# A fused attention and maxout kernel on one core: the order of batch 0's scores, weight transposes and block products, and the PSUM banks of its first up blocks

## The chip, the cores and the metric

The kernel runs on one NeuronCore of a Trainium2 chip. The metric is the device time in microseconds (us) of one execution, as a median over runs. A core has a matrix engine (TensorE, "PE" in the profile, with its weight loads as "PEld"), a vector engine (VectorE, "DVE"), an activation engine (ScalarE, "ACT"), GpSimd ("POOL", which here issues the loads), and SyncE ("SP", which issues stores and small DMAs). Each engine works through its own instructions in the order in which the program gives them; semaphores hold one back until another engine's result is there. TensorE writes only to PSUM, of which the kernel uses eight banks.

## The reference, cut to what matters

Eight batches of Linformer attention (keys and values are projected from 1024 positions to 64), followed by a maxout layer without biases:

```python
k_proj = np.einsum('ks,bhsd->bhkd', E, k)          # 8 batches, 8 heads, 1024 positions, 64 wide
v_proj = np.einsum('ks,bhsd->bhkd', F, v)
scores = scale * np.matmul(q, k_proj.transpose(0, 1, 3, 2))
attn   = softmax(scores)                            # over the 64 projected positions
x      = np.matmul(attn, v_proj)                    # then rows of 512: (8192, 512)
out    = np.maximum(x @ w1, x @ w2) @ w_out         # w1, w2: 512 x 1024; w_out: 1024 x 512
```

The kernel uses max(a, b) = relu(a - b) + b: with wd = w1 - w2 and M = w2 @ w_out it computes relu(x @ wd) @ w_out + x @ M. Most of the large products are done by a seven-product scheme for 2x2 blocks (Winograd's form of Strassen's), with sums of blocks made on VectorE.

## The kernel before, in words

The order of the work is written out by hand; no scheduler moves anything. Batches 1 to 7 run in a steady pipeline. All that the change touches is batch 0's start, whose steps stand in one list (L992 to L1041), followed by a list of small functions called `slots` (L1069 to L1082), which runs before the steady pipeline.

**The start.** Batch 0's heads are worked on in two groups g (four heads each) and two halves j of the positions. For each (g, j) the steps are: `step_sc` (scores: eight matmuls at L343 into two PSUM banks, then Exp on ACT, L383), `step_dn` (sums of the exponentials, eight matmuls at L355, then Ln on ACT, L391), `step_inv` (Exp of minus that, L430, and a small DMA), and `step_at` (the values: sixteen matmuls at L355, then two multiplications on DVE, L446, which write `xt`, the rows x of the reference turned on their side). `step_kv(..., "v")` projects v, 16 matmuls for every two heads (L197); the projection of heads 4 to 7 is copied to `vp` by ACT (L209), those of heads 0 to 3 by DVE. The loads of v come in four DMAs of two heads each. `warm(n)` are n matmuls without a use.

**The up blocks.** `up_slots(t, j)` (L519) gives eight blocks fb for each half j, here called u0[fb] and u1[fb]. One is four matmuls of 128x512 (L528, r = 0 to 3, of which r = 0, 1 need the head group g = 0 and r = 2, 3 need g = 1) into one PSUM bank, and then a relu out of the bank: on ACT at L537, for fb = 3 on DVE at L539. The first two blocks of each half are done in two pieces: the pieces r = 0, 1 of u0[0], u1[0], u0[1], u1[1] in this order (L1038), later the pieces r = 2, 3 of u0[0], u0[1], then of u1[0], u1[1] (L1070 to L1072).

**w2 on its side.** `step_w2t(f0)` (L556) transposes eight 128x128 pieces of w2 on TensorE (L560) into one bank, and ACT copies 128x1024 of them to `w2t_sb` (L568). There are four such steps; that of f0 = 768 leaves its copy for later (`box["w2t"]`).

**The seven-product parts.** S1, S2, S6, S5, S7, S3, S4 are the products of the second half of the up blocks of half 1 (L766); M1 to M4 are those of M (L644). DVE makes their block sums (L607, L719), wd (L544, L552) and the additions.

**PSUM banks.** Four banks are named mm0 to mm3, and two pairs form the rotating buffer "att". `mm_bank()` without a number takes the first of the list `turn` and puts it at the end; with a number it takes that bank. A new tile in a bank waits until the last reader of the bank's previous tile is done. By the time of L1037 `turn` is [0, 1, 2, 3], so that `first_banks` gives u0[0] and u0[1] the banks 0 and 1, u1[0] and u1[1] the banks 2 and 3. Every later up block takes bank fb % 2 (L524):

```python
t["up", j, fb] = mm_bank(n=first_banks[j][fb] if r1 < NDC else fb % 2)
```

S1 takes bank 2, S2 takes bank 3, M2 takes bank 0 and M5 bank 1.

Of the kernel before, what the change touches and what calls it, by code (L numbers as in the profile page):

```python
# [10 lines left out]
FP16 = mybir.dt.float16  # L11
# [8 lines left out]
def kernel(  # L20
# [12 lines left out]
    nc = tc.nc  # L33
# [29 lines left out]
    turn = [0, 1, 2, 3]  # L63

    def mm_bank(dtype=FP32, n=None):
        if n is None:
            n = turn.pop(0)
            turn.append(n)
        return ps.tile([128, 512 if dtype == FP32 else 1024], dtype, tag=f"mm{n}", name="mm_ps")

    def att_banks(dtype=FP32):
        return ps.tile(
            [128, 2, 512 if dtype == FP32 else 1024], dtype, tag="att", bufs=2, name="att_ps"
        )
# [4 lines left out]
    def big(n, dtype=FP16):  # L79
        return const.tile([128, 16384 // mybir.dt.size(dtype) // 2], dtype, tag=f"big{n}", name=f"big{n}")  # L80
# [45 lines left out]
    w2_sb = big(2).rearrange("p (r f) -> p r f", r=NDC)  # L126
    wo_sb = const.tile([128, NFB, DM], FP16, tag="wo", name="wo_sb")
    for g in range(2):
        for w_sb, w in ((w2_sb, moe_w2), (w1_sb, moe_w1)):
            nc.gpsimd.dma_start(  # L130
                out=w_sb.rearrange("p (g z) f -> p g z f", z=2)[:, g, :, 0:256],
                in_=w.rearrange("(g p z) f -> p g z f", p=128, z=2)[:, g, :, 0:256],
            )
    for w_sb, w, f0, f1 in (
# [3 lines left out]
        for z in range(2):  # L138
            nc.gpsimd.dma_start(
                out=w_sb.rearrange("p (g z) f -> p g z f", z=2)[:, :, z, f0:f1],  # L140
                in_=w.rearrange("(g p z) f -> p g z f", p=128, z=2)[:, :, z, f0:f1],
# [16 lines left out]
    ident16 = const.tile([128, 128], FP16)  # L158
# [26 lines left out]
    def step_kv(t, h0=0, h1=H, which="kv", att=False, dma=False, copy=nc.vector.tensor_copy, between=None):  # L185
        kv_ps = att_banks()[:, 0, :] if att else mm_bank(n=0 if dma else None)
        n = (h1 - h0) * D
        both = which == "v"
        nh = 2 if both else h1 - h0
        for h in range(0, h1 - h0, nh):  # L190
            if h and between is not None:
                between()
            for c in range(NC):
                for w in which:
                    i = "kv".index(w)
                    for r in range(2) if both else (i,):
                        nc.tensor.matmul(  # L197
                            out=kv_ps[r * KP : (r + 1) * KP, h * D : (h + nh) * D],
                            lhsT=eft[i][:, c, :],
                            rhs=t[w][:, h0 + h : h0 + h + nh, c, :],  # L200
                            start=(c == 0), stop=(c == NC - 1),
                        )
        zd = lambda ap: ap.rearrange("p (h d z) -> p h z d", d=D // 2, z=2)
        if "k" in which:
            eng = nc.vector.tensor_copy if which == "k" or dma else nc.scalar.copy
            kp = t["kp"][:, h0:h1]
            eng(out=kp[:, :, 0, :], in_=kv_ps[0:KP, 0:n].rearrange("p (h d) -> p h d", d=D))
        if both:
            copy(out=t["vp"][:, h0:h1], in_=zd(kv_ps[:, 0:n]))  # L209
        elif "v" in which:  # L210
            def finish_v():
                nc.vector.tensor_copy(out=t["vp"][KP:128, h0:h1], in_=zd(kv_ps[KP:128, 0:n]))
                if dma:
                    nc.vector.tensor_copy(out=kp[:, :, 1, :], in_=kp[:, :, 0, :])
                    step_kpt_dma(t)
                else:
                    step_vp(t, h0, h1)

            if att:
                return finish_v  # L220
            finish_v()


    def step_vp(t, h0=0, h1=H):
        fl = lambda ap: ap[:, h0:h1].rearrange("p h z d -> p (h z d)")
        nc.vector.tensor_copy(out=fl(t["vp"][0:KP]), in_=fl(t["vp"][KP:128]))
# [71 lines left out]
    def step_kpt_dma(t):  # L298
        nc.sync.dma_start_transpose(
            out=t["kpt"], in_=t["kp"].rearrange("p h r d -> p (h r d)")  # L300
        )
# [60 lines left out]
    def sums_into(t, g, j, dn_ps):  # L362
        tiles_into(lambda o: dn_ps[:, o, :], t["ex", g, j], lambda rows, hh: ones16[rows, 0:Z])
# [15 lines left out]
    def step_sc(t, g, j):  # L379
        sc_ps = att_banks()  # L380
        t["ps", g, j] = sc_ps
        score(t, g, j, [sc_ps[:, e, :] for e in range(2)])
        nc.scalar.activation(out=t["ex", g, j], in_=sc_ps, func=ACTF.Exp, scale=scale)  # L383

    def step_dn(t, g, j):
        dn_ps = t.pop(("ps", g, j))[:, :, 0:W]
        sums_into(t, g, j, dn_ps)
        ld = (ppool.tile([128, 2, W], FP32, tag="pd", bufs=4, name="ld_sb") if t is tiles[0]
              else soft.tile([128, 2, W], FP32, tag="soft", name="ld_sb"))
        t["ld", g, j] = ld  # L390
        nc.scalar.activation(out=t["ld", g, j], in_=dn_ps, func=ACTF.Ln)  # L391
# [36 lines left out]
    def step_inv(t, g, j):  # L428
        ld = t["ld", g, j]
        nc.scalar.activation(out=ld, in_=ld, func=ACTF.Exp, scale=-1.0)  # L430
        check(ld)
# [84 lines left out]
    w2t_sb = big(3).rearrange("p (f m) -> p f m", f=NFB)  # L516
# [32 lines left out]
    def step_wd_rows(f0):  # L549
        for z in range(2):  # L550
# [2 lines left out]
                out=rows(wd_sb), in0=rows(w1_sb), in1=rows(w2_sb), op=ALU.subtract  # L553
            )

    def step_w2t(f0, att=False, hold=False):  # L556
        ps_t = att_banks(FP16)[:, 0, :] if att else mm_bank(FP16)
        for f in range(2):
            for r in range(NDC):
                nc.tensor.transpose(  # L560
                    out=ps_t[:, (f * NDC + r) * 128 : (f * NDC + r + 1) * 128],
                    in_=w2_sb[:, r, f0 + f * 128 : f0 + (f + 1) * 128],
                    identity=ident16,
                )
        fb = f0 // 128

        def copy():
            nc.scalar.copy(  # L568
                out=w2t_sb[:, fb : fb + 2, :].rearrange("q f m -> q (f m)"), in_=ps_t
            )  # L570

        if hold:
            box["w2t"] = copy
        else:
            copy()
# [9 lines left out]
    CH = DM // 2  # L585
    units = [(b, o) for b in range(B) for o in range(2)]
    last = len(units) - 1
    U = {(b, o): {"n": n, "b": b, "o": o, "t": tiles[b]} for n, (b, o) in enumerate(units)}
# [4 lines left out]
    box = {}  # L593
# [15 lines left out]
    def step_t(part, which=range(4)):  # L609
        n0, n1, src = ((0, NG, wo_sb), (NG, NG + NX, m_sb))[part]  # L610
        hs = n1 - n0
        sub4(
            [T_sb[:, i, n0:n1, :] for i in range(4)],
            lambda h, c: src[:, h * hs : (h + 1) * hs, c * CH : (c + 1) * CH], which,
        )
# [6 lines left out]
    def sums_m(i):  # L622
        m_sums[i] = ppool.tile([128, NG, CH], FP16, tag="pd", bufs=4, name="p_sb")
        sum_s(lambda j, h: m_blk(j, h), lambda n: m_sums[n], i)
# [100 lines left out]
    def sums_x(u, which):  # L725
        step_s(u, x_blk, lambda i: s_x(i, u), which)

    def sums_g(u, which):
        step_s(u, g_blk, s_g, which)
# [262 lines left out]
    t = tiles[0]  # L992
# [26 lines left out]
    warm(2)  # L1019
    step_sc(t, 1, 0)  # L1020
    step_kv(t, 0, 2, "v")
    step_kv(t, 2, 4, "v")
    step_dn(t, 1, 0)
    step_sc(t, 1, 1)
    step_at(t, 0, 0)
    step_at(t, 0, 1)
    step_inv(t, 1, 0)
    step_kv(t, 4, 8, "v", True, copy=nc.scalar.copy, between=lambda: step_dn(t, 1, 1))
    step_inv(t, 1, 1)
    att_banks()  # L1030
    for f0 in (0, 128):
        step_wd(f0, 0, 2, 128)
    step_at(t, 1, 0, True)
    u0, u1 = [*up_slots(t, 0)], [*up_slots(t, 1)]
    step_wd(0, 2, 4)
    step_at(t, 1, 1, True)
    first_banks = turn[0:2], turn[2:4]  # L1037
    for i in range(2):  # L1038
        for u in u0, u1:
            u[i](r1=2)  # L1040
    step_w2t(0, True)  # L1041


    load_all(tiles[1], 1, "k", k)
# [1 line left out]
    wd = [lambda f0=f0: step_wd_rows(f0) for f0 in range(0, DF, 256)]  # L1046
    f = lambda s, *a: lambda: s(tiles[0], *a)

    def loads(b, *names):
# [17 lines left out]
    S1, S2, S6, S5, S7, S3, S4 = up_steps(U[0, 1], (1,))  # L1067
    M1, M2, M6, M5, M7, M3, M4, M_add = m_steps()
# [2 lines left out]
        lambda: step_w2t(256, True),  # L1071
        lambda: u1[0](r0=2), lambda: u1[1](r0=2), wd[1], lambda: sums_x(U[0, 1], range(4)),  # L1072
        u0[2], u0[3], S1, S2, lambda: step_w2t(512, True), lambda: step_w2t(768, True, True), wd[2],
        u0[4], u0[5], lambda: box.pop("w2t")(), wd[3],
        lambda: [step_tw(i, 1) for i in range(2)] and None, lambda: U[0, 1]["c0"](),
        lambda: [step_tw(i, 1) for i in range(2, 4)] and None,
        u1[4], S6, u1[5], S5, u0[6], S7, u0[7],
        lambda: [sums_m(i) for i in range(4)] and None, S3, S4,
        lambda: step_t(0, (0, 1)), M1, lambda: step_t(0, (2, 3)), M2, lambda: sums_x(U[0, 0], (0, 1)),
        M6, lambda: sums_g(U[0, 0], (0, 1)), M_add, M5, lambda: sums_g(U[0, 0], (2, 3)), M7, M3, M4,  # L1080
        lambda: (open_box(3), new_attn(tiles[1]), turn.__setitem__(slice(None), [2, 3])) and None,
    ]  # L1082
# [32 lines left out]
    t = tiles[1]  # L1115
    for n, x in enumerate((
# [4 lines left out]
        for name in x.split():  # L1121
# [6 lines left out]
            else:  # L1128
                g, j = int(name[2]), int(name[3])
# [14 lines left out]
    t = tiles[2]  # L1144
# [8 lines left out]
    for b in range(3, B):  # L1153
        t = tiles[b]
# [25 lines left out]
    for n, (b, o) in enumerate(units):  # L1180
# [14 lines left out]
        if n:  # L1195
            end = ("U", n - 1, 1, 6) if n > 1 else ("P", 0, 6, 1)
            m = 0 if n == last else 2
# [17 lines left out]
    for key, slot in slots:  # L1215
        r = slot()
        pending = [g for g in [r, *(f() for f in pending)] if g is not None]
        for s in steps.pop(key, ()):
            r = s()
# [5 lines left out]
    for reg in regs:  # L1225
# [4 lines left out]
        out=mm_bank()[0:1, 0:1], lhsT=ones16[:, 0:1], rhs=ones16[:, 0:1], start=True, stop=True  # L1230
# [166 lines left out]
```

## Time and profile before

| what | value |
|---|---|
| median of 3 runs | 319.62 us (319.59 to 319.87) |
| the profiled execution's own time | 319.29 us |
| its span (first to last instruction) | 317.5 us |
| granted TensorE clock, mean | 0.999 |
| PE busy | 311.7 us (98%) |
| PEld busy | 254.9 us (80%) |
| DVE busy | 244.9 us (77%) |
| ACT busy | 206.9 us (65%) |

The profile is of one execution. A row of its timeline gives the start in us from the span's start, the time to the end of the last of the instructions that it merges, the engine, the source line, the operation, output<-input, the shape and the count; in brackets stands how long the engine was idle before it, and what released it. Matmuls are pipelined, so that a row's time overlaps the next row's start; what one matmul costs is read from the starts. A busy engine is not an engine at its peak.

### The profile page before, as it was taken

Reading aid. Unit: us, or ns where it says so; the run is one execution under the profiler, and the core shown is the slowest. Engines: PE = TensorE matmul, PEld = TensorE weight load, DVE = VectorE, ACT = ScalarE, POOL = GpSimd, SP = SyncE. Lnnn points to the kernel's source line nnn. Section 1 sums busy time; section 2 is a strip of 40 time slices with the busy share of each in tenths; the row PEclk is TensorE's granted clock in tenths of the full one; section 3 lists DMA queues with packets and bytes.
Section 4 is the critical chain, followed back from the end, with each engine's and each line's share of the span. In section 5 each row is a group of like instructions: output and inputs, shape, how many; then the busy total and the mean of one; then the engine's idle time right before and its main releaser. Section 6 shows DMA issues by size and latency. Waiting matters only on the chain.

```text
span 317.5 us, 9309 instructions
## 1 busy us (share of the span) xinstructions
PE 311.7 (98%) x3902; PEld 254.9 (80%) x3902; DVE 244.9 (77%) x474; ACT 206.9 (65%) x375; POOL 39.7 (13%) x63
## 2 busy tenths in 40 slices
PE   7989999999999999999999999999999999999996
PEld 3656688788887888788887888788887888888885
DVE  3368997977969696996969696996969696969883
ACT  2477843767776777477776777476776777765541
POOL 8269002011000400003000300003000000000000
PEclk9999999999999999999999999999999999999999
DMA  8999999999978799997999699987998431313134
GB/s 190 206 201 199 207 206 202 208 166 165 185 144 193 135 195 245 235 190 118 226 242 243 124 199 246 218 164 124 224 222 204 90 101 36 103 34 102 35 102 136
DMA packets 76685, 53.72 MB, mean 169 GB/s; under 512 B 29664, under 2 KB 76128, under 8 KB 76640
## 3 DMA queue, kind: packets, MB, share of 16 engines
q0 software_dynamic: 30688, 28.05, 56.2%
q1 hardware_dynamic: 45664, 24.85, 31.5%
q8 instruction: 31, 0.51, 0.7%
q10 hardware_dynamic: 288, 0.20, 0.2%
q14 instruction: 14, 0.11, 0.1%
HBM read 57.15 MB, written 16.78 MB: 233 GB/s over the span
## 4 chain that ended last, share of the span: by engine, by line
PE 92%; DMA 5%; POOL 1%; ACT 1%; issue 0%; DVE 0%; POOLq 0%
PE mm_ps L874 47%; PE mm_ps L766 28%; DMA v_sb<-in_v_dram 4%; PE att_ps L355 3%; PE mm_ps L528 3%; PE mm_ps L197 3%; PE mm_ps L343 2%; PE att_ps L239 1%; PE att_ps L644 1%; PE mm_ps L644 1%; DMA out_dram<-o_sb 1%; PE mm_ps L313 1%; PE att_ps L560 1%; POOL k_sb L108 0%; POOL q_sb L108 0%; ACT ld_sb L391 0%
## 5 line engine op out<-in xcount | busy, mean ns | idle before, releaser
L736 ACT COPY p_sb<-mm_ps 128x512 f32<-128x512 f32 x180 | 102.4, 592 | 47.3 <-PE mm_ps L766 27.2
L874 PEld LDWEIGHTS <-big 128*128 128x128 f16 x768 | 73.5, 98 | 11.8 <-issue 3.6
L874 PE MATMUL mm_ps<-T_sb,big 128*128 128x256 f16 x576 | 76.9, 273 | 0.0
L781 DVE TENSOR_TENSOR gt_sb<-mm_ps,p_sb 128x512 f16<-128x512 f32 x58 | 39.9, 688 | 42.8 <-PE mm_ps L766 41.4
L766 PE MATMUL mm_ps<-big,big 128*128 128x256 f16 x348 | 52.2, 273 | 0.0
L766 PEld LDWEIGHTS <-big 128*128 128x128 f16 x464 | 45.4, 98 | 5.9 <-DVE big L607 0.2
L874 PE MATMUL mm_ps<-wo_sb,gt_sb 128*128 128x256 f16 x256 | 42.6, 273 | 0.0
L874 PEld LDWEIGHTS <-gt_sb 128*128 128x128 f16 x376 | 35.7, 98 | 6.7 <-issue 2.7
L472 ACT ACTIVATE ex_sb<-mm_ps 128x512 f16<-128x512 f32 x50 | 27.2, 596 | 18.0 <-PE mm_ps L343 12.3
L766 PEld LDWEIGHTS <-wd_sb 128*128 128x128 f16 x348 | 34.1, 98 | 4.4
L766 PE MATMUL mm_ps<-xt_sb,wd_sb 128*128 128x256 f16 x232 | 33.8, 273 | 0.0
L502 DVE TENSOR_TENSOR xt_sb<-att_ps,ld_sb 128x1024 f16<-128x1024 f32 x26 | 31.7, 1218 | 0.2
L874 PE MATMUL mm_ps<-m_sb,xt_sb 128*128 128x256 f16 x128 | 24.5, 273 | 0.0
L905 DVE TENSOR_TENSOR o_sb<-mm_ps,p_sb 128x512 f32<-128x512 f32 x32 | 21.8, 683 | 2.8 <-ACT p_sb L934 2.0
L784 DVE TENSOR_SCALAR gt_sb<-gt_sb 128x512 f16<-128x512 f16 (+1 forms) x62 | 21.8, 351 | 2.1
L305 POOL COPY junk<-qt_sb 1x1 f16<-1x1 f16 x6 | 1.4, 238 | 174.1 <-DMA qt_sb<-q_sb 174.1
L719 DVE TENSOR_TENSOR big<-gt_sb 128x1024 f16<-128x1024 f16 x32 | 21.8, 682 | 0.0
L874 PE MATMUL mm_ps<-wo_sb,big 128*128 128x256 f16 x128 | 21.5, 273 | 0.0
L843 ACT ACTIVATE gt_sb<-mm_ps 128x512 f16<-128x512 f32 x29 | 17.4, 600 | 5.9 <-PE mm_ps L766 5.9
L874 PE MATMUL mm_ps<-T_sb,gt_sb 128*128 128x256 f16 x120 | 20.3, 273 | 0.0
L781 DVE TENSOR_TENSOR gt_sb<-p_sb 128x512 f16<-128x512 f32 x29 | 19.8, 682 | 0.6 <-ACT p_sb L736 0.6
L874 PEld LDWEIGHTS <-xt_sb 128*128 128x128 f16 x188 | 18.3, 98 | 2.3 <-issue 0.2
(123 smaller groups left out, 432.9 us busy)
## 6 DMA issues: line engine op xcount, KB each, us to landing
out_dram<-o_sb SPq DMA_DIRECT2D x62, 256.0 KB
k_sb<-in_k_dram POOLq DMA_DIRECT2D x7, 1024.0 KB, 10.2
v_sb<-in_v_dram POOLq DMA_DIRECT2D x7, 1024.0 KB, 17.0
q_sb<-in_q_dram POOLq DMA_DIRECT2D x5, 1024.0 KB, 23.5
q_sb<-in_q_dram POOLq DMA_DIRECT2D x6, 512.0 KB, 16.1
big<-in_moe_w_dram POOLq DMA_DIRECT2D x12, 128.0 KB, 6.5
v_sb<-in_v_dram POOLq DMA_DIRECT2D x4, 256.0 KB, 13.4
wo_sb<-in_moe_w_out_dram POOLq DMA_DIRECT2D x1, 1024.0 KB, 10.3
```

Source lines behind the costliest of these rows:

```text
L197: nc.tensor.matmul(out=kv_ps[r * KP : (r + 1) * KP, h * D : (h + nh) * D], lhsT=eft[i][:, c, :], rhs=t[w][:, h0 + h : h0 + h + nh, c, :], ...
L355: nc.tensor.matmul(out=dst(r ^ (hh % 2))[hh * Z : (hh + 1) * Z, :], lhsT=weights(rows, hh), rhs=ex[rows, hh % 2, hh // 2 * W : (hh // 2 + ...
L472: nc.scalar.activation(out=t["ex", g, j][:, e, :], in_=banks[e], func=ACTF.Exp, scale=scale)
L502: nc.vector.tensor_tensor(out=x_out(t, g, j).rearrange("q z o n -> q o z n"), in0=at_ps.rearrange("q o (z n) -> q o z n", z=2), in1=ld[:, ...
L719: nc.vector.tensor_tensor(out=S(i), in0=S(0) if x is None else x, in1=y(), op=op)
L736: copy(out=x, in_=bank)
L766: nc.tensor.matmul(out=bank[:, m * W : (m + 1) * W], lhsT=w_[:, n_, (2 * d + m) * 128 : (2 * d + m + 1) * 128], rhs=a[:, n_, :], start=(n ...
L781: nc.vector.tensor_tensor(out=c_blk(j, c), in0=two(x), in1=two(y), op=ALU.add)
L784: nc.vector.tensor_scalar_max(ap, ap, 0.0)
L843: nc.scalar.activation(out=out, in_=in_, func=ACTF.Relu)
L874: nc.tensor.matmul(out=bank[i][:, 0:CH] if two_banks else bank[:, i * CH : (i + 1) * CH], lhsT=a(c)[:, i * 128 : (i + 1) * 128], rhs=w_(c) ...
L905: nc.vector.tensor_tensor(out=o_sb, in0=two(x), in1=two(y), op=ALU.add)
```

## The change

Lines are of the changed kernel where marked with +. It does four things to batch 0.

1. The scores of (1, 1) are moved ahead of the projection of v's heads 2 and 3; their sums (`step_dn(t, 1, 1)`) are moved from the middle of the projection of heads 4 to 7 to ahead of it. On ACT the Exp of (1, 1) thereby comes ahead of the Ln of (1, 0).
2. The eight transposes of `step_w2t(0)` are split in two halves by the rows of w2. The first four (`step_w2t_half(0, ...)`) are issued right after the last projection of v, into bank mm0; ACT's copy of them comes after the Exp of `step_inv(t, 1, 1)`. The other four stand where all eight stood.
3. `first_banks` becomes banks 1 and 2 for u0[0], u0[1], and 3 and 0 for u1[0], u1[1].
4. In `slots`, u1[4] and u1[5] come ahead of S6, the others of that stretch follow in another order, S3 comes after M1 and S4 after M2; ACT's held copy of w2's transposes comes after u1[4] instead of after u0[5].

The numbers of matmuls, transposes, DMAs and DVE instructions stay as they are. One 128x1024 copy on ACT becomes two of 128x512. The instructions on POOL and SP keep their order.

```diff
+    def step_w2t_half(g, ps_t):
+        for f in range(2):
+            for z in range(2):
+                r = 2 * g + z
+                nc.tensor.transpose(
+                    out=ps_t[:, (f * 2 + z) * 128 : (f * 2 + z + 1) * 128],
+                    in_=w2_sb[:, r, f * 128 : (f + 1) * 128], identity=ident16,
+                )
+        return lambda: nc.scalar.copy(
+            out=w2t_sb[:, 0:2, g * CH : (g + 1) * CH],
+            in_=ps_t[:, 0 : 2 * CH].rearrange("q (f m) -> q f m", f=2),
+        )
+
...
     step_sc(t, 1, 0)
     step_kv(t, 0, 2, "v")
+    step_sc(t, 1, 1)
     step_kv(t, 2, 4, "v")
     step_dn(t, 1, 0)
-    step_sc(t, 1, 1)
     step_at(t, 0, 0)
     step_at(t, 0, 1)
     step_inv(t, 1, 0)
-    step_kv(t, 4, 8, "v", True, copy=nc.scalar.copy, between=lambda: step_dn(t, 1, 1))
+    step_dn(t, 1, 1)
+    step_kv(t, 4, 8, "v", True, copy=nc.scalar.copy)
+    w2t_copy = step_w2t_half(0, mm_bank(FP16, turn[0]))
     step_inv(t, 1, 1)
+    w2t_copy()
     att_banks()
...
-    first_banks = turn[0:2], turn[2:4]
+    first_banks = turn[1:3], (turn[3], turn[0])
     for i in range(2):
         for u in u0, u1:
             u[i](r1=2)
-    step_w2t(0, True)
+    step_w2t_half(1, att_banks(FP16)[:, 0, :])()
...
-        u0[4], u0[5], lambda: box.pop("w2t")(), wd[3],
+        u0[4], u0[5], wd[3],
...
-        u1[4], S6, u1[5], S5, u0[6], S7, u0[7],
-        lambda: [sums_m(i) for i in range(4)] and None, S3, S4,
-        lambda: step_t(0, (0, 1)), M1, lambda: step_t(0, (2, 3)), M2, lambda: sums_x(U[0, 0], (0, 1)),
+        u1[4], lambda: box.pop("w2t")(), u1[5], S6, u0[6], S5, u0[7], S7,
+        lambda: [sums_m(i) for i in range(4)] and None,
+        lambda: step_t(0, (0, 1)), M1, S3, lambda: step_t(0, (2, 3)), M2, S4, lambda: sums_x(U[0, 0], (0, 1)),
```

## The prediction

> **What bounds the kernel now.** I read the page first, then the busy times of a long stretch, then TensorE's waits behind the start.
>
> ```profile
> span 317.5 us, 9309 instructions
> PE 92%; DMA 5%; POOL 1%; ACT 1%; issue 0%; DVE 0%; POOLq 0%
> ```
>
> The chain of work that ended last is TensorE for 92% of the span. The 5% DMA lie at the start (v) and at the end (the last store). The busy times from 22.60 to 308.60 us (columns: stretch, its length, busy us of PE, PEld, DVE, ACT, POOL, granted clock, DMA) and all waits of PE behind 22.7 us show how tight that is:
>
> ```profile
> 22.60:308.60 286.00, 285.99 (x3578) 238.16 (x3579) 231.45 (x426) 194.45 (x356) 27.20 (x41) 1.00 0.88 168
> ```
>
> ```profile
> PE mm_ps L1229 <- DMA out_dram<-o_sb: 1.2, 1, 1.2
> PE att_ps L355 <- ACT vp_sb L209: 0.5, 1, 0.5
> ```
>
> PE is busy for 285.99 of 286.00 us at full clock, and waits only for v's cast (before 22.61) and for the last store. So whatever moves PE after 22.61 us moves the end by as much: a microsecond of new wait is a microsecond of time, since no old wait is left to take it up. What can be gained lies in three things only: the start at 22.61, the 0.47 us wait ahead of it, and the work behind it.
>
> The start on PE, in order of time:
>
> ```profile
> 18.77 0.64 PE L197 MATMUL mm_ps<-v_sb,eft 128*64 128x128 f16 x16 [0.45 <-DMA v_sb<-in_v_dram]
> 19.34 0.30 PE L355 MATMUL att_ps<-ex_sb,ones 64*32 64x256 f16 x8
> 19.57 0.41 PE L343 MATMUL att_ps<-qt_sb,kpt_sb 64*64 64x256 f16 x8
> 19.91 0.63 PE L355 MATMUL mm_ps<-ex_sb,vp_sb 64*32 64x256 f16 x32
> 20.47 0.64 PE L197 MATMUL att_ps<-v_sb,eft 128*64 128x128 f16 x16
> 21.27 0.30 PE L355 MATMUL att_ps<-ex_sb,ones 64*32 64x256 f16 x8 [0.16 <-ACT ex_sb L383]
> 21.50 0.64 PE L197 MATMUL att_ps<-v_sb,eft 128*64 128x128 f16 x16
> 22.61 0.63 PE L355 MATMUL att_ps<-ex_sb,vp_sb 64*32 64x256 f16 x32 [0.47 <-ACT vp_sb L209]
> 23.21 1.90 PE L528 MATMUL mm_ps<-xt_sb,wd_sb 128*128 128x512 f16 x8
> 24.95 0.61 PE L560 MATMUL att_ps<-ident,big 128*128 128x128 f16 x8
> 25.39 1.03 PE L528 MATMUL mm_ps<-xt_sb,wd_sb 128*128 128x512 f16 x4
> 26.26 0.61 PE L560 MATMUL att_ps<-ident,big 128*128 128x128 f16 x8
> 26.70 2.75 PE L528 MATMUL mm_ps<-xt_sb,wd_sb 128*128 128x512 f16 x12
> 29.29 1.04 PE L766 MATMUL mm_ps<-xt_sb,wd_sb 128*128 128x256 f16 x8
> ```
>
> Starts give the prices: eight transposes cost 25.39 - 24.95 = 0.44 us, one 128x512 matmul (29.29 - 26.70) / 12 = 0.216. The last row holds the second pieces of u1[0] and u1[1] (four matmuls), then u0[2] and u0[3]; u0[2] starts at 26.70 + 4 x 0.216 = 27.56.
>
> **Part 1, scores and sums moved.** The scores of (1, 1) fill the 0.45 us wait for v ahead of 18.77 (their row takes 0.34 from start to start), and their Exp on ACT no longer holds up the sums at 21.27. What is late next are the loads of v, VectorE's copy of v, and VectorE itself:
>
> ```profile
> 19.01 0.71 POOL L139 DMA_DIRECT2D big<-in_moe_w_dram  x1 [1.41 <-DMA v_sb<-in_v_dram]
> 21.54 0.71 POOL L139 DMA_DIRECT2D big<-in_moe_w_dram  x1 [0.62 <-DMA v_sb<-in_v_dram]
> ```
>
> ```profile
> 19.45 0.29 DVE L209 CAST vp_sb<-mm_ps 128x128 f16<-128x128 f32 x1 [0.79 <-PE mm_ps L197]
> 20.47 2.48 DVE L446 TENSOR_TENSOR xt_sb<-mm_ps,ld_sb 128x512 f16<-128x512 f32 x4 [0.73 <-PE mm_ps L355]
> 22.87 0.48 DVE L544 TENSOR_TENSOR wd_sb<-big,big 128x256 f16<-128x256 f16 x2
> 24.80 1.28 DVE L446 TENSOR_TENSOR xt_sb<-att_ps,ld_sb 128x512 f16<-128x512 f32 x2
> ```
>
> POOL went on at 19.01 for the same load that let PE go at 18.77, so it is 0.24 late; the last pair of v, for which POOL waited until 21.54, then landed at about 21.30. Its projection ran at 21.50, so this end gains 0.20 at most. The values of (0, 0) need v's copy, done at 19.45 + 0.29 = 19.74; with 0.06 for the hand-over (ACT's cast of 22.18 + 0.37 = 22.55 let PE go at 22.61; its row stands below) they start at 19.80 instead of 19.91. VectorE's multiplications follow 0.56 behind (19.91 to 20.47) and then run without a gap to 26.08 (24.80 + 1.28), so all of them come 0.11 earlier. u0[0] needs the first wd of 22.87 and thus also starts 0.11 earlier, at 23.10. I take -0.11; the bounds are 0 (v's copy comes no sooner) and -0.20 (v's landing).
>
> **Part 2, four transposes moved.** They go from PE's full stretch into the wait ahead of the values of (1, 0): -0.22. They fit: four take 0.22 us, the wait has 0.47. u0[0]'s second piece then starts at 25.39 - 0.11 - 0.22 = 25.06. The eight transposes of w2t(256) would start at 25.93, but their bank is read by the multiplications that end at 26.08 - 0.11 = 25.97; with a hand-over of 0.05 they start at 26.02, 0.24 earlier than now. Without any other change u0[2] would then start at 27.32.
>
> **Part 3, the banks.** This is the term that decides. u1[1] now sits in bank 0, and u0[2] takes bank fb % 2 = 0 as before. Until now bank 0 held u0[0], whose relu is the first in ACT's order; now it holds u1[1], whose relu is the fourth, behind the 128x1024 copy of w2t(256). In the built programs u0[2]'s first matmul waits for ACT's 17th counted instruction before, u0[0]'s relu, and for the 22nd after, u1[1]'s; ACT's order is half copy, half copy, relu of u0[0] and u0[1], copy of w2t(256), relu of u1[0] and u1[1]. ACT now:
>
> ```profile
> 22.18 0.37 ACT L209 CAST vp_sb<-att_ps 128x256 f16<-128x256 f32 x1
> 22.45 0.63 ACT L430 ACTIVATE ld_sb<-ld_sb 128x512 f32<-128x512 f32 x1
> 25.59 1.01 ACT L568 COPY big<-att_ps 128x1024 f16<-128x1024 f16 x1 [2.51 <-PE att_ps L560]
> 26.50 1.09 ACT L537 ACTIVATE gt_sb<-mm_ps 128x512 f16<-128x512 f32 x2
> 27.47 1.03 ACT L568 COPY big<-att_ps 128x1024 f16<-128x1024 f16 x1
> 28.36 1.62 ACT L537 ACTIVATE gt_sb<-mm_ps 128x512 f16<-128x512 f32 x3
> ```
>
> The rows give: PE's end to ACT's start 0.20 (the transposes' last slot ends at 25.39, the copy starts at 25.59); a 128x1024 copy takes 0.89 to the next start (27.47 to 28.36), two relus 0.97 (26.50 to 27.47), one relu 0.60 to its end (1.09 for two that start 0.49 apart). The second half's transposes end at 25.06, so:
>
> - second half copy starts at 25.26. No row has a 128x512 copy of f16. Between the 128x256 cast (0.27 from 22.18 to the next start at 22.45) and the 128x1024 copy (0.89) I take the 0.49 of the 128x512 relus, which have its size: next start 25.75. With 0.27 the relu would still wait for PE, until 25.06 + 0.43 + 0.20 = 25.69; with 0.89 it starts at 26.15. So -0.06 or +0.40.
> - relus of u0[0], u0[1]: 25.75 + 0.97 = 26.72. The copy's transposes end at 26.02 + 0.44 = 26.46, and with 0.20 that is 26.66: no wait.
> - copy of w2t(256): 26.72 + 0.89 = 27.61.
> - relu of u1[0]: 27.61; of u1[1]: 28.10, to its end 28.70; hand-over 0.06: u0[2] starts at 28.76.
>
> Against 27.56 that is **+1.20 us**; PE stands still for 28.76 - 27.32 = 1.44. Behind u0[2] in PE's queue is all the rest, and no wait is left that takes it up.
>
> If bank 0's copy of the first half were late it would hold u1[1]'s first piece; it starts behind the Exp of (1, 1), at about 22.8, and has until 23.10 + 6 x 0.216 = 24.40. No cost.
>
> **Part 4, the new order.** It removes no wait, because PE has none there now. It adds round trips: u1[5] now directly follows u1[4] and waits for bank 1, which u0[5]'s relu frees.
>
> ```profile
> 31.06 2.75 PE L528 MATMUL mm_ps<-xt_sb,wd_sb 128*128 128x512 f16 x12
> 32.99 0.60 ACT L537 ACTIVATE gt_sb<-mm_ps 128x512 f16<-128x512 f32 x1 [0.27 <-PE mm_ps L528]
> ```
>
> u0[5] ends at 31.06 + 8 x 0.216 = 32.79; its relu runs to 33.59 and with 0.06 the bank is free 0.86 behind the block's end, which is just the time of the block between (4 x 0.216). u1[4] does the same now without a wait, so I put 0, with +0.05 as the other end. ACT's held copy comes two relus later, and the sums of w2 on VectorE behind it:
>
> ```profile
> 34.98 0.69 DVE L719 TENSOR_TENSOR p_sb<-big 128x1024 f16<-128x1024 f16 x1
> 38.23 0.69 DVE L607 TENSOR_TENSOR T_sb<-wo_sb,T_sb 128x1024 f16<-128x1024 f16 x1
> 40.17 1.04 PE L644 MATMUL att_ps<-T_sb,p_sb 128*128 128x256 f16 x8
> ```
>
> With PE 1.20 later, u1[4] ends at 33.65 + 1.20 = 34.85 (33.65 is where the row of 31.06 ends by starts), its relu starts at 35.05, the copy at 35.54 and ends near 36.5; VectorE's sums start 1.5 later than 34.98, so 0.3 later against PE. M6 at 40.17 has 1.25 us to spare behind T's row (38.92): cover enough. Without it, 0.3.
>
> **Sum.** -0.11 - 0.22 + 0.09 (bank of w2t(256)) + 1.44 = +1.20. The profiled execution took 319.29 us for a span of 317.5 (1.79 around it): 318.7 + 1.79 = 320.5. It lies 0.33 under the median of the runs; the median becomes 319.62 + 1.20 = 320.8.
>
> **The rivals.**
>
> 1. *The bank is free in time (not slower).* One mechanism, at L524: if u1[1]'s relu ends by 27.26, u0[2] doesn't wait, and -0.11 - 0.22 + 0.09 = -0.24 remains: 319.4 us. It decides from 1.44 us on: so much shorter must ACT's row from the half copy to u1[1]'s relu be. For it speaks that ACT is idle before 25.59 for 2.51 us; against it that the five instructions ahead can't start before their matmuls of 25.06 to 26.46, and that the rows leave 0.06 us of air in 3.5. This is also the case in which the change does what its words say and nothing else. 8 in 100.
> 2. *The clock falls in the new wait.* PE's opening shows what a slow clock costs:
>
> ```profile
> 1.47 3.60 PE L153 MATMUL mm_ps<-ones 128*128 128x512 f16 x8 [1.47 <-DVE ones L146]
> 5.00 1.14 PE L169 MATMUL mm_ps<-ident,big 64*128 64x64 f32 x8
> ```
>
> Eight matmuls take 3.53 us there by starts, 0.44 each, against 0.216 later, so a repetition costs 3.53 - 8 x 0.216 = 1.8: 322.6 us. Against it: the wait of 0.47 us just ahead of 22.61 was followed by a clock of 1.00 in the row of the long stretch. No row shows a wait of 1.4. 4 in 100.
>
> The Trainium skill, "TensorE: Matmul & The Clock Gate", section "What's actually happening", says that the array's clock is halved after an idle window of about 3.4 us. By that rule a wait of 1.44 us is too short, and this rival doesn't come; no run here shows yet whether that holds for such a wait.
>
> 3. *ACT's queue is shorter or longer than I lay it out,* by a copy of another price or a relu that starts otherwise: a part of the stall, some +0.3 (319.9), 4 in 100; or with the round trips of part 4 and the slow half copy +1.7 (321.3), inside the range.
>
> **How the numbers follow.** Forecast 320.8, 81 in 100 with its own spread; rival 1 8, rival 2 4, a part of the stall 4, something longer 3. The range takes -0.09 (front gain of 0.20) and +0.40 + 0.05 + 0.11 from the unknown costs, widened at the low end for the hand-overs read from single rows: 320.3 to 321.4. About 0.2% (0.64 us) is what a measurement of this kernel can tell from no change. Within it fall rival 1 and the part of a stall: 0.11. Faster by more would need over 0.64, and parts 1 and 2 together hold 0.42 at most: 0.01. Slower: 0.88.
>
> **What would show it.** In the profile of the changed kernel PE has one new wait of about 1.4 us ahead of L528 (u0[2]), released by ACT's relu of L537, near 28.8 us; from there all PE rows lie 1.2 us later. The four moved transposes stand ahead of the values of (1, 0), whose start is near 22.45. Wrong would be: no such wait (rival 1), 128x512 matmuls at 0.44 us behind it (rival 2), or a wait of PE later on, which I exclude.

## The result, and the profile after

The changed kernel takes 321.24 us (median of 6 runs, 321.20 to 321.47) against 319.64 us before (6 runs, 319.57 to 320.12): 1.60 us or 0.46% slower, ratio 1.0046 with a 95% interval of 1.0036 to 1.0056. The profiled execution took 321.24 us for a span of 319.5. The forecast was 320.8, with a range of 320.3 to 321.4.

The page of the changed kernel, and its waits of PE behind 22.3 us (columns: who waited for what, us in total, times, longest):

```profile
span 319.5 us, 9309 instructions
PE 90%; DVE 3%; DMA 3%; ACT 2%; issue 1%; DVEq 0%; POOLq 0%; ACTq 0%
```

```profile
PE mm_ps L528 <- ACT gt_sb L537: 1.2, 1, 1.2
PE mm_ps L1245 <- DMA out_dram<-o_sb: 1.2, 1, 1.2
PE mm_ps L528 <- DVE wd_sb L544: 0.2, 1, 0.2
PE att_ps L657 <- ACT p_sb L749: 0.2, 1, 0.2
```

Lines behind L554 are shifted: L574 to L779 stand for L561 to L766 of the kernel before, and so on (L657 is M's products, L749 the copies to `p_sb`, L887 the units' products). The 0.5 us wait for v's cast is gone from the list, as the change says. Three waits are new: up blocks for ACT's relu, the first up block for wd, and M's products for a copy of ACT. The one for wd costs nothing by itself: the first up block starts 0.33 us behind the start of the first wd on VectorE (23.13 to 23.46), as it did before by 0.34 (22.87 to 23.21); PE only has less to do ahead of it. The chain, 92% PE before, now passes through DVE and ACT. PE's rows show where they lie:

```profile
22.20 0.40 PE L560 MATMUL mm_ps<-ident,big 128*128 128x128 f16 x4
22.65 0.63 PE L355 MATMUL att_ps<-ex_sb,vp_sb 64*32 64x256 f16 x32
23.46 1.90 PE L528 MATMUL mm_ps<-xt_sb,wd_sb 128*128 128x512 f16 x8 [0.18 <-DVE wd_sb L544]
25.20 0.39 PE L560 MATMUL att_ps<-ident,big 128*128 128x128 f16 x4
25.43 1.03 PE L528 MATMUL mm_ps<-xt_sb,wd_sb 128*128 128x512 f16 x4
26.49 0.61 PE L573 MATMUL att_ps<-ident,big 128*128 128x128 f16 x8
26.93 1.03 PE L528 MATMUL mm_ps<-xt_sb,wd_sb 128*128 128x512 f16 x4
29.18 1.89 PE L528 MATMUL mm_ps<-xt_sb,wd_sb 128*128 128x512 f16 x8 [1.23 <-ACT gt_sb L537]
...
44.40 1.04 PE L657 MATMUL mm_ps<-wo_sb,p_sb 128*128 128x256 f16 x8
45.61 1.03 PE L657 MATMUL att_ps<-T_sb,big 128*128 128x256 f16 x8 [0.16 <-ACT p_sb L749]
46.48 0.60 PE L887 MATMUL mm_ps<-wo_sb,gt_sb 128*128 128x256 f16 x4
```

The bracket counts idle time from the modelled end of the matmul before. By starts, u0[2] would have come at 26.93 + 4 x 0.216 = 27.79 and comes at 29.18: 1.39 us. The last product of M would have come at 44.40 + 0.87 and comes at 45.61: 0.34 us.

ACT's rows show what the first of the two waits for, and what the second:

```profile
25.62 0.58 ACT L564 COPY big<-att_ps 128x512 f16<-128x512 f16 x1 [2.02 <-PE att_ps L560]
26.11 1.09 ACT L537 ACTIVATE gt_sb<-mm_ps 128x512 f16<-128x512 f32 x2
27.13 1.01 ACT L581 COPY big<-att_ps 128x1024 f16<-128x1024 f16 x1
28.04 1.09 ACT L537 ACTIVATE gt_sb<-mm_ps 128x512 f16<-128x512 f32 x2
...
35.96 1.01 ACT L581 COPY big<-att_ps 128x1024 f16<-128x1024 f16 x1
...
44.97 0.58 ACT L749 COPY p_sb<-att_ps 128x512 f32<-128x512 f32 x1 [0.65 <-DVE m_sb L670]
```

The second of the two relus from 28.04 (u1[1]) ends at 28.04 + 1.09 = 29.13, and u0[2] starts 0.05 later. For the second wait one has to go one step further back, to VectorE:

```profile
20.73 2.48 DVE L446 TENSOR_TENSOR xt_sb<-mm_ps,ld_sb 128x512 f16<-128x512 f32 x4 [0.60 <-PE mm_ps L355]
...
25.06 1.28 DVE L446 TENSOR_TENSOR xt_sb<-att_ps,ld_sb 128x512 f16<-128x512 f32 x2
...
37.00 0.69 DVE L732 TENSOR_TENSOR p_sb<-big 128x1024 f16<-128x1024 f16 x1 [1.34 <-ACT big L581]
...
44.19 0.68 DVE L670 TENSOR_TENSOR m_sb<-mm_ps,p_sb 128x512 f16<-128x512 f32 x1
```

VectorE waits 1.34 us for ACT's held copy (35.96 + 1.01 = 36.97), starts w2's sums at 37.00 instead of 34.98, and comes to M_add (L670) at 44.19 instead of 42.17: 2.0 later, where PE is only 1.6 later. M is made of seven products too, in the order M1, M2, M6, M5, M7, M3, M4, and M_add is the addition that takes M1 and M2. M_add is the last reader of M1's copy, one of three buffers; M7's copy needs that buffer (44.97, released by m_sb), and the last product of M goes into the bank from which M7's copy reads. In the kernel before, M_add and M7's copy were these rows:

```profile
42.17 0.69 DVE L657 TENSOR_TENSOR m_sb<-mm_ps,p_sb 128x512 f16<-128x512 f32 x1
42.99 0.59 ACT L736 COPY p_sb<-att_ps 128x512 f32<-128x512 f32 x1 [0.29 <-PE att_ps L644]
```

One number sums up each kernel below, called the stretch: the time on PE from the first up block (first row of L528) to the first product of unit 0 (L887, before the change L874), which is the first one behind M. In the kernel before that is this row:

```profile
44.54 0.60 PE L874 MATMUL mm_ps<-wo_sb,gt_sb 128*128 128x256 f16 x4
```

The stretch is 44.54 - 23.21 = 21.33 us before and 46.48 - 23.46 = 23.02 after: +1.69.

### The profile page after: what moved, and what is told of

Read it like the earlier page. It is cut to its first block, busy times and chain, and to the rows that moved or that the text cites. A ratio compares the mean times of both kernels' runs of the same rounds, so it can differ in the third digit from the quotient of the medians.

```text
span 319.5 us, 9309 instructions
## 1 busy us (share of the span) xinstructions
PE 312.9 (98%) x3902; PEld 254.9 (80%) x3902; DVE 244.4 (77%) x474; ACT 207.1 (65%) x376; POOL 39.5 (12%) x63
## 4 chain that ended last, share of the span: by engine, by line
PE 90%; DVE 3%; DMA 3%; ACT 2%; issue 1%; DVEq 0%; POOLq 0%; ACTq 0%
PE mm_ps L887 47%; PE mm_ps L779 27%; PE mm_ps L197 4%; PE att_ps L355 3%; PE mm_ps L343 2%; DMA k_sb<-in_k_dram 2%; PE mm_ps L528 2%; PE att_ps L239 1%; PE mm_ps L313 1%; PE mm_ps L153 1%; ACT gt_sb L537 1%; DVE T_sb L620 1%; DVE p_sb L732 1%; DMA out_dram<-o_sb 1%; PE att_ps L343 1%
## 5 line engine op out<-in xcount | busy, mean ns | idle before, releaser
L749 ACT COPY p_sb<-mm_ps 128x512 f32<-128x512 f32 x180 | 102.4, 592 | 48.1 <-PE mm_ps L779 28.0
L887 PEld LDWEIGHTS <-big 128*128 128x128 f16 x768 | 73.5, 98 | 11.8 <-issue 3.6
L887 PE MATMUL mm_ps<-T_sb,big 128*128 128x256 f16 x576 | 76.9, 273 | 0.0
L779 PE MATMUL mm_ps<-big,big 128*128 128x256 f16 x348 | 52.2, 273 | 0.0
L779 PEld LDWEIGHTS <-big 128*128 128x128 f16 x464 | 45.4, 98 | 5.9
L887 PE MATMUL mm_ps<-wo_sb,gt_sb 128*128 128x256 f16 x256 | 42.6, 273 | 0.0
L887 PEld LDWEIGHTS <-gt_sb 128*128 128x128 f16 x376 | 35.7, 98 | 6.7 <-issue 2.7
L779 PEld LDWEIGHTS <-wd_sb 128*128 128x128 f16 x348 | 34.0, 98 | 4.2
L779 PE MATMUL mm_ps<-xt_sb,wd_sb 128*128 128x256 f16 x232 | 33.8, 273 | 0.0
L887 PE MATMUL mm_ps<-m_sb,xt_sb 128*128 128x256 f16 x128 | 24.4, 273 | 0.0
L887 PE MATMUL mm_ps<-wo_sb,big 128*128 128x256 f16 x128 | 21.5, 273 | 0.0
L887 PE MATMUL mm_ps<-T_sb,gt_sb 128*128 128x256 f16 x120 | 20.3, 273 | 0.0
L887 PEld LDWEIGHTS <-xt_sb 128*128 128x128 f16 x188 | 18.3, 98 | 2.3 <-issue 0.2
```

Source lines behind the costliest of these rows:

```text
L749: copy(out=x, in_=bank)
L779: nc.tensor.matmul(out=bank[:, m * W : (m + 1) * W], lhsT=w_[:, n_, (2 * d + m) * 128 : (2 * d + m + 1) * 128], rhs=a[:, n_, :], start=(n ...
L887: nc.tensor.matmul(out=bank[i][:, 0:CH] if two_banks else bank[:, i * CH : (i + 1) * CH], lhsT=a(c)[:, i * 128 : (i + 1) * 128], rhs=w_(c) ...
```

## The experiments

The theory after the result, called A in the expectations: u0[2] waits for the relu of u1[1], whose bank it takes over, through all that stands ahead of it on ACT; beside it the late held copy delays M. Rival B: the moved start loses the time. Rival C: the new order of the products does. The table sets each kernel beside the kernel before, as a median of runs of the same chip. A difference between two versions is surer by the stretch, which leaves out when the loads of the opening landed.

| kernel | median us | before, same chip | ratio, 95% interval | stretch on PE, us |
|---|---|---|---|---|
| e1: banks back | 319.82 | 319.59 | 0.9998 to 1.0016 | 21.62 |
| e2: banks alone | 321.60 | 319.59 | 1.0044 to 1.0072 | 23.30 |
| e3: old order of products | 320.77 | 319.59 | 1.0021 to 1.0045 | 22.69 |
| e4: new order alone | 319.90 | 319.59 | 1.0001 to 1.0019 | 21.66 |
| e5: banks and order back | 319.52 | 319.64 | 0.9987 to 1.0009 | 21.30 |
| e6: banks back, copy early | 319.79 | 319.64 | 0.9992 to 1.0011 | 21.39 |
| e7: banks back, addition early | 319.65 | 319.64 | 0.9986 to 1.0027 | 21.30 |
| e8: transposes alone | 319.60 | 319.64 | 0.9988 to 1.0006 | 21.30 |
| e9: e5, second half later | 319.45 | 319.56 | 0.9993 to 1.0012 | 21.30 |
| e10: copy behind relus | 320.18 | 319.56 | 1.0009 to 1.0027 | 22.07 |

**e1, the banks taken back in the changed kernel.**

```diff
-    w2t_copy = step_w2t_half(0, mm_bank(FP16, turn[0]))
+    w2t_copy = step_w2t_half(0, mm_bank(FP16, turn[1]))
-    first_banks = turn[1:3], (turn[3], turn[0])
+    first_banks = turn[0:2], turn[2:4]
```

> The changed kernel, but the four early transposes go to bank 1 and the first up blocks have the banks of the kernel before again (u0: 0 and 1, u1: 2 and 3). Theory A (u0[2] waits for the fourth relu, that of u1[1], because it shares its bank): the wait of 1.2 us ahead of L528 goes, u0[2] follows u1[1] at once, and the time falls by about 1.4 us to 319.8 to 319.9; the wait of about 0.3 us ahead of the last product of M stays. Rival B (the moved scores and transposes make the start late): the time stays at 321.0 or more, and the rows of the up blocks start as late as in the changed kernel. Rival C (the new order of the block products costs it): the time falls by less than 0.4 us.

319.82 us. In PE's rows u1's second pieces, u0[2] and u0[3] are one row again, and the wait of M's last product stays:

```profile
26.83 2.75 PE L528 MATMUL mm_ps<-xt_sb,wd_sb 128*128 128x512 f16 x12
...
44.12 1.03 PE L657 MATMUL att_ps<-T_sb,big 128*128 128x256 f16 x8 [0.17 <-ACT p_sb L749]
```

The banks were worth 321.24 - 319.82 = 1.42 us (1.40 by the stretch: 23.02 - 21.62). That excludes B as the main cause, and C with more than about 0.3.

**e2, the banks alone changed in the kernel before** (only the line of `first_banks`).

> The kernel before, with the change of the banks alone (u0: 1 and 2, u1: 3 and 0). Theory A: u0[2] waits for the relu of u1[1], which in the kernel before ends near 29.45 us, so that it starts near 29.5 instead of 27.56; the time rises by 1.9 us to 321.5. Rivals B and C: no measurable difference, 319.6.

321.60 us, 2.01 over before. PE waits longer than in the changed kernel, since here two full copies of 128x1024 stand ahead of u1[1]'s relu on ACT:

```profile
29.86 1.89 PE L528 MATMUL mm_ps<-xt_sb,wd_sb 128*128 128x512 f16 x8 [1.81 <-ACT gt_sb L537]
```

```profile
28.68 1.13 ACT L537 ACTIVATE gt_sb<-mm_ps 128x512 f16<-128x512 f32 x2
```

28.68 + 1.13 = 29.81, and u0[2] starts at 29.86. One line of the change, put into the kernel before, costs more than the whole change.

**e3, the old order of the block products in the changed kernel** (the four lines of `slots` as before).

> The changed kernel with the old order of the block products and of the held copy of w2's transposes; banks and start as changed. Theory A with its second term (VectorE's sums of w2 come late behind the held copy, so that the copy of M7 and with it the last product of M wait 0.33 us): 321.24 - 0.33 = 320.9, and the wait ahead of the last product of M is gone, that ahead of u0[2] stays at 1.2 us. Rival B: 321.2. Rival C: back to 319.9 or less.

320.77 us, 0.47 under the changed kernel (0.33 by the stretch). The wait of M's last product is gone (from 44.30 to 45.17 there is one product's time), that ahead of u0[2] stays:

```profile
29.08 1.89 PE L528 MATMUL mm_ps<-xt_sb,wd_sb 128*128 128x512 f16 x8 [1.23 <-DVE big L732]
```

```profile
27.93 1.09 ACT L537 ACTIVATE gt_sb<-mm_ps 128x512 f16<-128x512 f32 x2
```

The row names a sum of VectorE as the releaser. In the built program u0[2]'s first matmul waits for ACT's counter alone, and ACT's relu ends at 27.93 + 1.09 = 29.02, 0.06 ahead. The sum of VectorE that lies nearest runs from 28.67 to 28.67 + 0.42 = 29.09, so that it ends with the start and not ahead of it. Here the releaser that the view infers is a neighbour in time, not the cause.

**e4, the new order alone in the kernel before.**

> The kernel before with the new order of the block products and the later held copy alone. Theory A with its second term: the sums of w2 start about 0.35 us later, the addition that frees the buffer for M7's copy too, and the last product of M waits some 0.3 us: 319.9 to 320.0. Rival B: 319.6. Rival C: 321 or more.

319.90 us, 0.31 over before, with the wait in its place and by the same buffer:

```profile
44.29 1.03 PE L644 MATMUL att_ps<-T_sb,big 128*128 128x256 f16 x8 [0.17 <-ACT p_sb L736]
```

```profile
43.65 0.59 ACT L736 COPY p_sb<-att_ps 128x512 f32<-128x512 f32 x1 [0.66 <-DVE m_sb L657]
```

So the wait does not need the stall ahead of u0[2]; the later held copy and the order are enough.

**e5, banks and order both taken back.** What is left of the change are the moved scores and sums and the early transposes.

> The changed kernel with the banks of the first up blocks as before (early transposes in bank 1) and with the old order of the block products: only the moved scores and sums and the four early transposes are left of the change. Theory A: neither the wait ahead of u0[2] nor that ahead of the last product of M; the front's gain is left, some 0.1 to 0.25 us: 319.82 - 0.33 = 319.5. Rival (the front loses): 319.8 or more.

319.52 us; neither wait is there. The gain over before isn't clear of the measurement.

**e6 and e7, which part of the new order makes the second wait.** Both start from e1. e6 puts ACT's held copy back behind u0[5]; e7 leaves the copy and moves M_add ahead of two sums:

```diff
-        M6, lambda: sums_g(U[0, 0], (0, 1)), M_add, M5, ...
+        M6, M_add, lambda: sums_g(U[0, 0], (0, 1)), M5, ...
```

> The changed kernel with the banks as before and with ACT's held copy of w2's transposes behind u0[5] again, the new order of the products otherwise kept. Theory A, second term by the late copy: the wait ahead of the last product of M goes, 319.5. Rival (the order of the products makes that wait, by S3 and S4 between M1 and M6): the wait stays, 319.8.

> The changed kernel with the banks as before and with VectorE's addition that frees the first of ACT's three buffers (M_add) ahead of two sums instead of behind them; held copy and order of the products as changed. If M7's copy waits for that buffer, as the trace of the changed kernel has it, the wait ahead of the last product of M goes although the sums of w2 come as late as there: 319.5, unless the two sums, now 0.6 us later, hold up the first products of unit 0. If not the buffer but the lateness of VectorE as a whole is the cause, the time stays at 319.8.

The medians (319.79 and 319.65) don't tell 0.3 us apart on that chip, where single runs of e7 went up to 324.06, e6's profiled execution took 321.62 (its opening, below) and e6's median is the 319.8 of its rival. The traces do: the list of PE's waits holds none for `p_sb` in either. In e6 M7's copy is released by PE again, and in e7 the last product of M follows the one before by 0.87:

```profile
45.24 0.59 ACT L749 COPY p_sb<-att_ps 128x512 f32<-128x512 f32 x1 [0.29 <-PE att_ps L657]
```

```profile
42.91 1.04 PE L657 MATMUL mm_ps<-wo_sb,p_sb 128*128 128x256 f16 x8
43.78 1.04 PE L657 MATMUL att_ps<-T_sb,big 128*128 128x256 f16 x8
```

So the wait is the buffer that M_add frees, and the late copy is what makes M_add late: either cure removes it. e6's stretch of 21.39 is 0.09 over e7's, because there the early copy delays the relu of u1[4], whose bank u0[6] takes: that block starts 0.52 us behind the start of S6 (36.68 to 37.20) instead of 0.44.

**e8, the early transposes alone in the kernel before** (in bank 1).

> The kernel before with the four early transposes alone (in bank 1, banks of the up blocks as before). By the steps of the prediction 0.22 us less work behind the start, of which the bank of w2t(256), read until VectorE's multiplications end, takes back what is over 0.13 us: 319.59 - 0.13 = 319.46. If the early transposes hold up the start of the values: 319.6 or more.

319.60 us, and a stretch of 21.30 against 21.33: 0.03 us gained, not 0.13. The time is also what the other case of the expectation names, but the values aren't held up: those of (1, 0) start 1.10 us behind the projection of the last heads (21.76 to 22.86), as in e4 (21.80 to 22.90), which lacks the transposes there. The transposes of w2t(256) wait for VectorE's last multiplications of the start:

```profile
26.51 0.61 PE L573 MATMUL att_ps<-ident,big 128*128 128x128 f16 x8
```

```profile
25.08 1.28 DVE L446 TENSOR_TENSOR xt_sb<-att_ps,ld_sb 128x512 f16<-128x512 f32 x2
```

They start 26.51 - 26.36 = 0.15 behind VectorE's end, as in the changed kernel (26.49 behind 25.06 + 1.28 = 26.34). In the kernel before it was 26.26 behind 26.08: 0.18, but there PE came to them no sooner (25.39 + 0.87 = 26.26).

**e9, the second half of the transposes moved into that wait** (e5, with `step_w2t_half(1, ...)` behind u0[1]'s second piece).

> Banks and order of the block products as before, moved scores and early transposes kept, and the second half of the transposes moved behind the second pieces of u0[0] and u0[1], into the time in which the transposes of w2t(256) wait for VectorE's multiplications. If that wait (0.19 us in the changed kernel) is what ate the gain of the early transposes, the stretch from the first up block to the first product of unit 0, 21.30 to 21.33 us in the kernels without other waits, becomes 21.1 to 21.2, and the time falls to 319.3 to 319.4. If not, 21.3 and 319.5.

A miss: 319.45 us, and the stretch stays 21.30. The four transposes now do fill PE, but w2t(256) still starts 0.15 behind the multiplications:

```profile
25.91 0.39 PE L560 MATMUL att_ps<-ident,big 128*128 128x128 f16 x4
26.33 0.61 PE L573 MATMUL att_ps<-ident,big 128*128 128x128 f16 x8
```

```profile
24.90 1.28 DVE L446 TENSOR_TENSOR xt_sb<-att_ps,ld_sb 128x512 f16<-128x512 f32 x2
```

24.90 + 1.28 = 26.18. At this point PE isn't the bound; VectorE's eight multiplications and three subtractions from 20.56 on are. They set the first up block, which waits for wd, as well as w2t(256): from the one to the other it is 3.02 or 3.03 us in e8, e9 and the changed kernel and 3.05 before, whatever PE does between.

**e10, less on ACT ahead of u1[1]'s relu,** with the changed banks.

```diff
-        lambda: step_w2t(256, True),
-        lambda: u1[0](r0=2), lambda: u1[1](r0=2), wd[1], ...
+        lambda: u1[0](r0=2), lambda: u1[1](r0=2), lambda: step_w2t(256, True), wd[1], ...
```

> The changed kernel, its banks and its order of the block products too, with the eight transposes of w2t(256) and with them ACT's 128x1024 copy moved behind the second pieces of u1[0] and u1[1]. Theory A (the wait ahead of u0[2] is the queue on ACT ahead of u1[1]'s relu, of which the copy is 0.9 us): u1[1]'s relu ends near 28.2 instead of 29.13, u0[2] waits about 0.5 us instead of 1.2, and the time falls by 0.9 to 320.3. If the sharing of the bank alone costs the wait, whatever ACT does ahead, the time stays at 321.2.

320.18 us, 1.06 under the changed kernel (0.95 by the stretch). u0[2] still waits, but less:

```profile
28.42 1.89 PE L528 MATMUL mm_ps<-xt_sb,wd_sb 128*128 128x512 f16 x8 [0.37 <-ACT gt_sb L537]
```

```profile
26.30 2.07 ACT L537 ACTIVATE gt_sb<-mm_ps 128x512 f16<-128x512 f32 x4
```

The fourth relu ends at 26.30 + 2.07 = 28.37, and u0[2] starts at 28.42. So the price of the shared bank is what ACT has queued ahead of the bank's last reader.

No version is faster than the kernel before by more than the measurement tells; the medians of e9, e5 and e8 lie 0.04 to 0.12 us under it, inside their intervals.

## Why the prediction was right, and where it was off

- *Every wait behind 22.61 counts in full:* right for both new waits. e2's stretch is 1.97 longer, its time 2.01; e4's 0.33 and 0.31.
- *Part 3, the bank, a wait of 1.44 us:* right in mechanism and size. 1.39 measured, and the half copy's distance to the next start, taken as 0.49, is 26.11 - 25.62 = 0.49. e1, e2 and e10 show it from three sides.
- *Part 4 at nothing, since M6 had 1.25 us to spare:* this step failed, and it is the term that was missed, +0.34. M6's cover was real (0.83 us were left of it: T's row ends at 40.26 + 0.69 = 40.95, and M6 starts at 41.78), but the prediction looked at M6 only. The reader of VectorE with next to nothing to spare was M7's copy on ACT, which takes the buffer that M_add frees. Before, M_add ended at 42.86 and that copy started at 42.99, released by PE. VectorE's shift against PE, foreseen as 0.3 that would cost 0.3 without cover, was 0.41 (37.00 - 34.98 = 2.02, where M7 on PE is 1.61 later) and cost 0.34. The round trips of u1[4] and u1[5] cost nothing, as put.
- *Part 2, -0.22 and +0.09 back for w2t(256):* too large by 0.10. 0.19 comes back (25.43 + 0.87 = 26.30 to 26.49), so that e8 gains 0.03. The mis-sized step is the hand-over from VectorE's end to these transposes, put at 0.05, measured as 0.15.
- *Part 1, -0.11:* right where v is late, which is not so in every execution. The starts of single executions don't show it: the first up block starts at 23.21 before, at 23.49 to 23.52 in e2, e4 and e8, which lack the moved scores as well, and at 23.31 to 23.65 in the kernels that have them (25.40 in e6), since the loads land at other times. So count from the row in which POOL goes on behind v's second load (19.01 before): the first up block starts 4.20 to 4.23 us behind it in the four kernels without the moved scores, and 4.07 to 4.10 in e1, e3, e7, e9 and e10. In the profiled executions of the changed kernel and of e5 it is 4.23 and 4.24. There PE's earlier work ran late, the moved scores were done only after v had landed (the projection starts 0.07 and 0.10 ahead of POOL's row instead of 0.24), and nothing was gained. The start of the profile before was an early one, with v's load 0.25 to 0.3 earlier than in e2, e4 and e8, which would account for its own time lying 0.33 under the median.
- *Sum:* from the first up block on the rows give -0.22 + 0.19 + 1.39 + 0.34 = 1.70, and the stretch 1.69. With the -0.11 of part 1 that is 1.59, measured 1.60; forecast 1.20. The whole difference is in the missed 0.34 and the 0.10 of part 2, less 0.05 of part 3.
- *The range:* that 321.24 lies inside it is in part luck. Its upper end had room for a slow half copy (+0.40), for round trips (+0.05) and for v (+0.11). The half copy and the round trips cost just what was taken for them, and it was the missed term that used up the room. A wait of PE later on, which the prediction excluded and named as a sign of being wrong, did come.
- *Rivals:* the bank that is free in time is excluded by the wait; the clock stayed at full speed behind the new wait, and behind e2's 1.81 us too: the eight matmuls behind it take 30.91 - 29.18 = 1.73 us here and 31.58 - 29.86 = 1.72 in e2, 0.216 and 0.215 each. (The prediction says that no row shows a wait of 1.4 us. Its row of 1.47 has one, but at the very start, ahead of all matmuls.)

## What to carry to other kernels

A list of PSUM banks is also a list of who waits for whom: when a tile is moved to another bank, look up which instruction reads that bank last and what stands ahead of it in its engine's queue; that queue is the price. When work on one engine is made later, ask of each of its results which reader has the least time to spare, buffers that it frees included, instead of the reader nearest at hand. A row of unbroken busy time on one engine doesn't show that it is the bound: here PE's transposes of w2t(256) started only 0.18 us behind VectorE's end, of which the hand-over takes 0.15, so that 0.22 us less work on PE gained 0.03.

## What the runs showed of the hardware

One thing wasn't expected. In e6's profiled execution two loads came late in the opening, so that PE waited 1.08 and 0.52 us within 3 us; the 5 us from 10 to 15 (columns as in the prediction's long stretch, the clock ahead of the last two) then ran at a granted clock of 0.66:

```profile
8.09 1.03 PE L197 MATMUL mm_ps<-k_sb,eft 128*64 128x256 f16 x8 [1.08 <-DMA k_sb<-in_k_dram]
9.64 1.07 PE L169 MATMUL mm_ps<-ident,big 64*128 64x64 f32 x8 [0.52 <-DMA big<-in_F_dram]
```

```profile
10.00:15.00 5.00, 5.00 (x52) 3.41 (x51) 1.68 (x3) 0.59 (x1) 1.41 (x2) 0.66 1.24 206
```

Taken by single microseconds the clock is 0.98, 0.50, 0.50, 0.50 and 0.82, so it was at half speed for about 3.4 us (an estimate from these five). That execution took 321.62 us, 1.83 over the kernel's median. So a single wait of 1.81 us between long runs of dense matmuls (e2) left the clock alone, while two shorter ones among small matmuls and transposes (L169) were followed by a slow stretch. By the idle window of about 3.4 us that the Trainium skill gives ("TensorE: Matmul & The Clock Gate", section "What's actually happening"), read as a time in which PE does nothing, neither should have slowed it; e2 agrees with that, e6 doesn't. Whether it is the share of busy time in a window that decides wasn't tried. The price of a matmul is a surer sign than the recorded clock: in the first 5 us of the kernel before the record reads 1.00, while eight 128x512 matmuls take 0.44 us each.
